# kv and M of a linear-attention block: from 6-head blocks on the whole array to 3-head blocks on 64-wide array tiles

## The chip, the cores and the metric

The kernel runs on one core of a Trainium2 chip. The metric is device time of one execution in microseconds (us); it is quoted as the median over runs. Engines in the profile: PE is TensorE's matmuls, PEld its weight loads, DVE VectorE, ACT ScalarE, POOL GpSimd, SP the engine that issues most DMAs (SPq is its queue). "Granted clock" is the share of TensorE's full clock in the records.

## The reference, cut to what matters

```python
def _A_ref(x, wqkv, wo):                     # B=1, S=2048, D=640, H=32 heads of 20
    q, k, v = ...                            # x @ wqkv, split into heads
    phi = lambda t: jnp.where(t > 0, t + 1, jnp.exp(t)) + 1e-6
    pq, pk = phi(q), phi(k)
    kv = jnp.einsum("bhsd,bhse->bhde", pk, v)      # 20 x 20 for each head
    z = jnp.einsum("bhsd->bhd", pk)
    o = jnp.einsum("bhqd,bhde->bhqe", pq, kv) / (den(pq, z) + 1e-6)
    return o @ wo
def _B_ref(x, w_gate, w_up, w_down):         # F = 1728
    return (gelu(x @ w_gate) * (x @ w_up)) @ w_down
g = sigmoid((x * gate_w).sum(-1, keepdims=True))
return g * _A_ref(...) + (1 - g) * _B_ref(...)
```

The kernel never forms `o`. It computes G = xᵀ·pk, then kv = wvᵀ·G for each head, then M = kv·wo (640 x 640), and puts (normalised pq)·M into the same accumulators as the FFN's last product. kv and M are the subject here. They are small: a head's kv is a 20 x 20 block on the diagonal of a 640 x 640 product.

## The kernel before: the parts that matter

Six heads (120 columns) are taken as one block. kv of a block is computed whole, 120 x 120, and everything off the 20 x 20 blocks is masked away. M of a block is one 120-row product in two halves of 320 columns. Its rows lie at multiples of 120, but the output stage wants them in tiles of 128 rows, so DMAs move them.

```python
    GH = 6; GW = GH * Dh; NG = 6             # 120 columns a block; the last block has 40
    def ps_tile(name):                       # one of the pool's 8 buffers (a "bank" below)
        return psum.tile([P, QW], FP32, name=name, tag="ps")
    ...
    def phase_KV(glo, ghi):
        kp = ps_tile("ps_kv")
        off = 0
        for g in range(glo, ghi):
            for ct in range(ND):             # ND = 5 tiles of 128 to contract over
                nc.tensor.matmul(
                    kp[0 : gw[g], off : off + gw[g]], lhsT=wv[:, ct, GW * g : GW * g + gw[g]],
                    rhs=g_sb[:, ct, GW * g : GW * g + gw[g]], start=(ct == 0), stop=(ct == ND - 1),
                )
            off += gw[g]
        ...                                  # kvt = kp * mask, on DVE
    def phase_M(g):
        ...
        for hh in range(2):
            cs = slice(hh * HALF, (hh + 1) * HALF)
            mp = ps_tile("ps_m")
            nc.tensor.matmul(mp[0 : gw[g], 0:HALF], lhsT=kvt[0 : gw[g], g, 0 : gw[g]],
                             rhs=wo_g[0 : gw[g], g, cs], start=True, stop=True)
            ...                              # cast to bf16: hh 0 on DVE, hh 1 on ACT
        ...                                  # 1 or 2 DMAs a block (10 in all) to rows of 128
    def phase_D(st):                         # normalise q, all on DVE, then a DMA transpose
        prod = work.tile([P, D], FP32, name="prod", bufs=2)
        nc.vector.tensor_tensor(out=prod[:], in0=pq[st][:], in1=zrep[:], op=ALU.mult)
        ...
    ...
    phase_Zrep()                             # the z product, "ps_z"
    phase_KV(0, 4)
    phase_E(1, 0)                            # FFN: 5 gate and 5 up matmuls, 128 x 512
    phase_KV(4, NG)
    ...
    phase_E(1, 1)
    phase_D(0)
    for ft in range(2, NF):
        phase_E(1, ft)
        if 0 <= ft - 3 < NG:
            phase_M(ft - 3)
        phase_D(ft - 1)
    for st in range(NF - 1, NT):
        phase_D(st)
    phase_FT(0)                              # first output stage: "ps_acc", then oT on DVE
```

## Time and profile before

| | before |
|---|---|
| time, median of the first 6 runs | 278.53 us (278.22 to 280.13) |
| PE busy, share of the span | 270.8 us, 98% |
| from the z product to the first output matmul (the "stretch" below) | 32.97 us |
| PE time of kv / of M in it | 1.69 us / 1.84 us |

The page's first and fourth parts say what bounds the kernel: busy us of each engine, and the shares of the chain of waits that ended last.

```profile
PE 270.8 (98%) x1462; PEld 136.5 (49%) x1487; DVE 146.9 (53%) x309; ACT 75.2 (27%) x155; POOL 3.7 (1%) x16
...
PE 96%; DMA 2%; issue 1%; SPq 0%; DVE 0%
```

PE is nearly always busy and is nearly the whole chain. What shortens PE's own work shortens the kernel, unless PE then has to wait.

The windows view of the stretch gives its length, then busy us (and instructions) of PE, PEld, DVE, ACT and POOL, then the granted clock, the DMA share and GB/s:

```profile
101.57:134.54 32.97, 32.76 (x178) 16.42 (x180) 31.81 (x63) 12.52 (x23) 0.00 (x0) 1.00 0.34 85
```

PE is busy 32.76 of 32.97 us, but DVE is too (31.81). DVE is the engine to watch for new waits.

The timeline of PE has one row per run of like instructions: start, us until the last one's modelled end, and what they are. To cost a stage, take starts alone, since the ends overlap with the next row. A 128x512 matmul starts 0.216 us after the one before it, so five take 1.08 us.

```profile
101.57 0.43 PE L262 MATMUL ps_z<-zsum,ones_bf 128*128 128x320 bf16 x2
101.84 1.26 PE L288 MATMUL ps_kv<-g_sb,wv 128*120 128x120 bf16 x20
102.94 1.24 PE L154 MATMUL ps_g<-xT_88,wg 128*128 128x512 bf16 x4
104.02 1.24 PE L154 MATMUL ps_u<-xT_88,wu 128*128 128x512 bf16 x5
105.10 0.66 PE L288 MATMUL ps_kv<-g_sb,wv 128*120 128x120 bf16 x10
105.69 0.60 PE L154 MATMUL ps_g<-xT_88,wg 128*128 128x512 bf16 x2
...
121.91 0.44 PE L316 MATMUL ps_m<-wo_g,kvt 120*120 120x320 bf16 x2
122.19 1.24 PE L154 MATMUL ps_g<-xT_88,wg 128*128 128x512 bf16 x4
123.27 1.24 PE L154 MATMUL ps_u<-xT_88,wu 128*128 128x512 bf16 x5
124.44 0.45 PE L316 MATMUL ps_m<-wo_g,kvt 40*40 40x320 bf16 x2
124.82 0.39 PE L154 MATMUL ps_g<-xT_88,wg 128*128 128x512 bf16 x1
```

kv: 101.84 to 102.94 and 105.10 to 105.69, together 1.69 us. M: a full block takes 0.27 to 0.28 us (121.91 to 122.19), five of them 1.37; the 40-row block takes from 123.27 + 1.08 = 124.35 to 124.82, 0.47 us, although its two matmuls need only 0.27. The other 0.2 us is lost where TensorE goes from 128*128 tiles to 40*40 ones and back: 0.09 us on each side (124.35 to 124.44 us, and 124.59 + 0.14 to 124.82). Sum: 3.53 us, 1.3% of the span. That is the ceiling of any change to kv and M.

### The profile page before, as it was taken

To read this page: it belongs to the slowest core of one execution; us is meant where nothing else is said; L and a number is where in the kernel's file an instruction comes from. 1 tells how busy PE (TensorE), PEld (TensorE's weight loads), DVE (VectorE), ACT (ScalarE), POOL (GpSimd) and SP (SyncE) were. 2 spreads that over 40 slices of the span, in tenths; PEclk is the share of its full clock that TensorE was granted. 3 is DMA by queue.
4 is the path that set the end of the run, shared out by engine and by line. 5 is a ranking of instruction groups with operands and counts; after the bars stand their busy time and mean duration, and the time that the engine had idled before them with its cause. 6 is when DMAs were issued, how large, how long until landed. Compare 5 with 4: busy or idle time off the path is not lost.

```text
span 277.1 us, 3820 instructions
## 1 busy us (share of the span) xinstructions
PE 270.8 (98%) x1462; PEld 136.5 (49%) x1487; DVE 146.9 (53%) x309; ACT 75.2 (27%) x155; POOL 3.7 (1%) x16
## 2 busy tenths in 40 slices
PE   7999999999999999999999999999999999999996
PEld 3554444555554494544444444444444444445675
DVE  0693323999998019999999863241122234111011
ACT  3572233644542252443100122220013222000100
POOL 4000000000000000000000000000000000000000
PEclk9999999999999999999999999999999999999999
DMA  6999999300000104343323352000132000011301
GB/s 199 357 357 202 241 350 279 128 0 2 0 0 4 1 2 137 68 105 77 61 47 45 74 99 95 2 0 19 38 40 95 0 0 2 19 38 34 125 24 47
DMA packets 43898, 23.64 MB, mean 85 GB/s; under 512 B 30825, under 2 KB 43753, under 8 KB 43881
## 3 DMA queue, kind: packets, MB, share of 16 engines
q1 hardware_dynamic: 43726, 23.25, 32.4%
q8 instruction: 11, 0.18, 0.3%
q10 hardware_dynamic: 154, 0.17, 0.2%
q14 instruction: 7, 0.05, 0.1%
HBM read 13.40 MB, written 2.63 MB: 58 GB/s over the span
## 4 chain that ended last, share of the span: by engine, by line
PE 96%; DMA 2%; issue 1%; SPq 0%; DVE 0%
PE ps_u L154 20%; PE ps_g L154 20%; PE ps_acc L363 15%; PE ps_kq L200 15%; PE ps_G L240 8%; PE ps_acc L360 6%; PE ps_acc L401 5%; PE ps_acc L398 2%; DMA wqk<-in_A_wqkv_dram 2%; PE ps_gu L154 2%; PE ps_k L200 1%; PE ps_acc L368 1%; PE ps_m L316 1%; PE ps_kv L288 1%; PE tp_x L145 0%
## 5 line engine op out<-in xcount | busy, mean ns | idle before, releaser
L159 ACT ACTIVATE gl<-ps_g 128x512 bf16<-128x512 f32 x52 | 31.1, 597 | 111.2 <-PE ps_g L154 111.2
L154 PEld LDWEIGHTS <-wu 128*128 128x128 bf16 x260 | 25.4, 98 | 30.7
L154 PEld LDWEIGHTS <-wg 128*128 128x128 bf16 x260 | 25.1, 98 | 29.1 <-issue 0.3
L160 DVE TENSOR_TENSOR hT_157<-ps_u,gl 128x512 bf16<-128x512 f32 x26 | 17.8, 689 | 29.5 <-PE ps_u L154 29.5
L363 PEld LDWEIGHTS <-wd 128*128 128x128 bf16 x195 | 19.1, 98 | 23.0
L363 PE MATMUL ps_acc<-hT_157,wd 128*128 128x512 bf16 x127 | 29.4, 379 | 0.2
L181 ACT ACTIVATE phi_e<-ps_kq 128x512 bf16<-128x512 f32 (+3 forms) x48 | 23.0, 505 | 21.2 <-PE ps_kq L200 19.1
L371 DVE TENSOR_TENSOR oT<-ps_acc,omg_rep 128x512 bf16<-128x512 f32 x15 | 10.4, 691 | 34.5 <-PE ps_acc L363 26.6
L160 DVE TENSOR_TENSOR hT_1249<-ps_u,gl 128x512 bf16<-128x512 f32 x26 | 17.8, 685 | 19.1 <-PE ps_u L154 19.1
L154 PE MATMUL ps_g<-xT_88,wg 128*128 128x512 bf16 x62 | 16.0, 379 | 0.2
L154 PE MATMUL ps_u<-xT_89,wu 128*128 128x512 bf16 x65 | 16.2, 379 | 0.0
L154 PE MATMUL ps_u<-xT_90,wu 128*128 128x512 bf16 x65 | 16.2, 379 | 0.0
L154 PE MATMUL ps_u<-xT_87,wu 128*128 128x512 bf16 x65 | 16.1, 379 | 0.0
L154 PE MATMUL ps_u<-xT_88,wu 128*128 128x512 bf16 x65 | 16.1, 379 | 0.0
L154 PE MATMUL ps_g<-xT_87,wg 128*128 128x512 bf16 x63 | 16.0, 379 | 0.1
L154 PE MATMUL ps_g<-xT_89,wg 128*128 128x512 bf16 x62 | 16.0, 379 | 0.2
L154 PE MATMUL ps_g<-xT_90,wg 128*128 128x512 bf16 x62 | 16.0, 379 | 0.2
L401 PE MATMUL ps_acc<-wd,hT_1249 128*128 128x320 bf16 (+2 forms) x120 | 15.9, 283 | 0.0
L240 PEld LDWEIGHTS <-x_all 128*128 128x128 bf16 x160 | 12.4, 98 | 7.1
L363 PE MATMUL ps_acc<-hT_1249,wd 128*128 128x512 bf16 x63 | 14.7, 379 | 0.1
L183 DVE TENSOR_SCALAR phi_m<-phi_e 128x512 bf16<-128x512 bf16 (+3 forms) x52 | 12.2, 258 | 2.1 <-ACT phi_e L181 1.9
L339 DVE TENSOR_REDUCE den<-prod 128x32 f32<-128x640 f32 x16 | 12.8, 801 | 0.0
(140 smaller groups left out, 290.8 us busy)
## 6 DMA issues: line engine op xcount, KB each, us to landing
wd<-in_B_w_down_dram SPq DMA_DIRECT2D x1, 2080.0 KB, 15.8
x_all<-in_A_x_dram SPq DMA_DIRECT2D x3, 640.0 KB, 5.9
out_dram<-o_q SPq DMA_DIRECT2D x3, 640.0 KB, 5.1
wg<-in_B_w_gate_dram SPq DMA_DIRECT2D x2, 640.0 KB
wu<-in_B_w_up_dram SPq DMA_DIRECT2D x2, 640.0 KB, 10.1
wqk<-in_A_wqkv_dram SPq DMA_DIRECT2D x1, 800.0 KB
wg<-in_B_w_gate_dram SPq DMA_DIRECT2D x1, 800.0 KB, 10.5
wu<-in_B_w_up_dram SPq DMA_DIRECT2D x1, 800.0 KB
```

What stands on the lines that cost most here:

```text
L154: nc.tensor.matmul(ps[:, t0 : t0 + tw], lhsT=w[:, dk, ft * P : (ft + 1) * P], rhs=xT[q][:, dk, t0 : t0 + tw], start=(dk == 0), stop=(dk == ...
L159: nc.scalar.activation(out=gl[:], in_=psg[:], func=ACT.Gelu_apprx_tanh)
L160: nc.vector.tensor_tensor(out=hT_cur[q][:, ft, :], in0=psu[:], in1=gl[:], op=ALU.mult)
L181: nc.scalar.activation(out=e[:, 0:w], in_=ps[:, 0:w], func=ACT.Exp)
L183: nc.vector.tensor_scalar(out=m[:, 0:w], in0=e[:, 0:w], scalar1=1.0, scalar2=EPS, op0=ALU.min, op1=ALU.add,)
L200: nc.tensor.matmul(ps[:, 0 : hi - lo], lhsT=xT[q][:, dk, sl * P : (sl + 1) * P], rhs=wqk[:, dk, lo:hi], start=(dk == 0), stop=(dk == ND - 1),)
L240: nc.tensor.matmul(gp[:, 0 : hi - lo], lhsT=x_all[:, st, ct * P : (ct + 1) * P], rhs=pk[st][:, lo:hi], start=(st == 0), stop=(st == NT - 1),)
L339: nc.vector.tensor_reduce(out=den[:], in_=prod[:].rearrange("p (h c) -> p h c", c=Dh), axis=AX.X, op=ALU.add)
L360: nc.tensor.matmul(acc[:], lhsT=M["all"][:, dk, ds], rhs=pqT[q][:, dk, :], start=(dt == 0 and dk == 0), stop=False)
L363: nc.tensor.matmul(acc[:], lhsT=wd[:, ft, ds], rhs=hT[:, ft, :], start=False, stop=(dt > 0 and ft == NF - 2))
L371: nc.vector.tensor_tensor(out=oT[:, 0:QW], in0=acc[:], in1=gsc["rep"][:, q * QW : (q + 1) * QW], op=ALU.mult)
L401: nc.tensor.matmul(acc[:, 0:w], lhsT=hT[:, ft, ts], rhs=wd[:, ft, lo:hi], start=False, stop=(ft == nf - 1 and (sl, h) != paired[0]))
```

## The change

Its intent: a 120-wide block wastes most of its kv (only 20 x 20 blocks are kept) and works the whole array (128*120 in the timeline). With 3-head blocks of 60, two kv matmuls are to run side by side in two column tiles of 64 (128*60), and four M matmuls (a quad) in four 64x64 tiles (60*64). The blocks of a pair of groups are laid out so that M's rows come out as whole blocks of 60. Fifteen DMAs instead of ten place them. kv is done in one piece, M in two lots, earlier than before. The core of the diff:

```diff
-    GH = 6
+    GH = 3
     GW = GH * Dh
     NG = 6
+    SUB = [(g, r, min(GW, D - GW * (2 * g + r))) for g in range(NG) for r in range(2) if GW * (2 * g + r) < D]
+    RP = P // 2
...
+    def phase_KV():
+        kps = [ps_tile("ps_kv") for _ in range(2)]
+        for g in range(NG):
             for ct in range(ND):
+                for gg, r, w in SUB:
+                    if gg == g:
+                        cs = slice(GW * (2 * g + r), GW * (2 * g + r) + w)
+                        nc.tensor.matmul(
+                            kps[r][RP * r : RP * r + w, GW * g : GW * g + w], lhsT=wv[:, ct, cs],
+                            rhs=g_sb[:, ct, cs], start=(ct == 0), stop=(ct == ND - 1),
+                        )
...
+    def phase_M(quads):
...
+        mps = {(q, r): ps_tile("ps_m") for q in quads for r in range(2)}
+        for pair, hh in quads:
+            for c in range(2):
+                for g, r, w in SUB:
+                    if g == 2 * pair + c:
+                        nc.tensor.matmul(
+                            mps[(pair, hh), r][RP * c : RP * c + RP, 0:HALF], lhsT=kvt[RP * r : RP * r + w, g, :],
+                            rhs=wo_g[RP * r : RP * r + w, g, hh * HALF : (hh + 1) * HALF], start=True, stop=True,
+                        )
...
-    phase_KV(0, 4)
     hT_cur[1] = ov.tile([P, NF, QW], BF16, name="hT1", tag="slab_b")
     phase_E(1, 0)
-    phase_KV(4, NG)
+    phase_KV()
...
-    phase_E(1, 1)
-    phase_D(0)
-    for ft in range(2, NF):
+    for ft in range(1, NF):
         phase_E(1, ft)
-        if 0 <= ft - 3 < NG:
-            phase_M(ft - 3)
-        phase_D(ft - 1)
-    for st in range(NF - 1, NT):
+        if ft == 1:
+            phase_M(((0, 0), (0, 1), (1, 0)))
+        elif ft == 2:
+            phase_M(((1, 1), (2, 0), (2, 1)))
+        else:
+            phase_D(ft - 3)
+    for st in range(NF - 3, NT):
         phase_D(st)
```

Cut: `wo_g` is loaded in two halves at partitions 0 and 64 (one DMA more), the mask and the zeroed `kvt` are made for 60-wide blocks, the casts of M go to ACT and DVE by `r`, and the placing DMAs.

More of the change, by code (lines that the diff above doesn't have):

```diff
@@ L42 @@
     HALF = D // 2
-    GH = 6
+    GH = 3
     GW = GH * Dh
     NG = 6
-    gw = [min(GW, D - GW * g) for g in range(NG)]
+    SUB = [(g, r, min(GW, D - GW * (2 * g + r))) for g in range(NG) for r in range(2) if GW * (2 * g + r) < D]
+    RP = P // 2
     NWARM = 6
@@ L78 @@
     wv = ov.tile([P, ND, D], BF16, name="wv", tag="slab_e")
-    wo_g = wpool.tile([GW, NG, D], BF16, name="wo_g")
+    wo_g = wpool.tile([P, NG, D], BF16, name="wo_g")
     wd = wpool.tile([P, NF, D], BF16, name="wd")
@@ L110 @@
     dma(out=wv[:], in_=wqkv_v[:, :, 2 * D : 3 * D])
-    dma(out=wo_g[:, 0 : NG - 1, :], in_=A_wo[0 : GW * (NG - 1), :].rearrange("(g p) n -> p g n", p=GW))
-    dma(out=wo_g[0 : gw[-1], NG - 1, :], in_=A_wo[GW * (NG - 1) : D, :])
+    wo_v = A_wo[0 : 2 * GW * (NG - 1), :].rearrange("(g r p) n -> r p g n", r=2, p=GW)
+    for r in range(2):
+        dma(out=wo_g[RP * r : RP * r + GW, 0 : NG - 1, :], in_=wo_v[r])
+    dma(out=wo_g[0 : SUB[-1][2], NG - 1, :], in_=A_wo[2 * GW * (NG - 1) : D, :])
     dma(out=wd[:, 0 : NF - 1, :], in_=B_w_down[0:FM, :].rearrange("(k p) n -> p k n", p=P))
@@ L120 @@
                          rhs=nc.const_aps.tensor(1.0, [P, QW], BF16), start=(r == 0), stop=(r == NWARM - 1))
-    NGB = 4
-    mask = consts.tile([GW, NGB * GW], BF16, name="mask")
+    mask = consts.tile([P, NG * GW], BF16, name="mask")
     nc.gpsimd.memset(mask[:], 1.0)
-    mv = mask[:].rearrange("p (g h c) -> p g h c", g=NGB, h=GH)
-    nc.gpsimd.affine_select(
-        out=mv, in_=mv, pattern=[[0, NGB], [-Dh, GH], [0, Dh]],
-        compare_op=ALU.is_ge, fill=0.0, base=0, channel_multiplier=1,
-    )
-    nc.gpsimd.affine_select(
-        out=mv, in_=mv, pattern=[[0, NGB], [Dh, GH], [0, Dh]],
-        compare_op=ALU.is_ge, fill=0.0, base=Dh - 1, channel_multiplier=-1,
-    )
+    for r in range(2):
+        mv = mask[RP * r : RP * r + RP, :].rearrange("p (g h c) -> p g h c", g=NG, h=GH)
+        nc.gpsimd.affine_select(
+            out=mv, in_=mv, pattern=[[0, NG], [-Dh, GH], [0, Dh]],
+            compare_op=ALU.is_ge, fill=0.0, base=0, channel_multiplier=1,
+        )
+        nc.gpsimd.affine_select(
+            out=mv, in_=mv, pattern=[[0, NG], [Dh, GH], [0, Dh]],
+            compare_op=ALU.is_ge, fill=0.0, base=Dh - 1, channel_multiplier=-1,
+        )
     eneg = consts.tile([P, NT], FP32, name="eneg")
@@ L279, in phase_gate @@
         gsc["omg"] = omg_all
-    kvt = consts.tile([GW, NG, GW], BF16, name="kvt")
-    def phase_KV(glo, ghi):
-        kp = ps_tile("ps_kv")
-        off = 0
-        for g in range(glo, ghi):
-            for ct in range(ND):
-                nc.tensor.matmul(
-                    kp[0 : gw[g], off : off + gw[g]], lhsT=wv[:, ct, GW * g : GW * g + gw[g]],
-                    rhs=g_sb[:, ct, GW * g : GW * g + gw[g]], start=(ct == 0), stop=(ct == ND - 1),
-                )
-            off += gw[g]
-        off = 0
-        full = [g for g in range(glo, ghi) if gw[g] == GW]
-        n = len(full)
+    kvt = consts.tile([P, NG, RP], BF16, name="kvt")
@@ new lines @@
+    nc.gpsimd.memset(kvt[:], 0.0)
+    def phase_KV():
+        kps = [ps_tile("ps_kv") for _ in range(2)]
+        for g in range(NG):
+            for ct in range(ND):
+                for gg, r, w in SUB:
[4 more added lines that the diff above has]
+                            rhs=g_sb[:, ct, cs], start=(ct == 0), stop=(ct == ND - 1),
+                        )
+        for r in range(2):
+            rs = slice(RP * r, RP * r + GW)
+            n = NG - 1
+            nc.vector.tensor_tensor(
+                out=kvt[rs, 0:n, 0:GW], in0=kps[r][rs, 0 : n * GW].rearrange("p (g c) -> p g c", g=n),
+                in1=mask[rs, 0 : n * GW].rearrange("p (g c) -> p g c", g=n), op=ALU.mult,
+            )
+        w = SUB[-1][2]
@@ L296, in phase_KV @@
         nc.vector.tensor_tensor(
-            out=kvt[:, glo : glo + n, :], in0=kp[0:GW, 0 : n * GW].rearrange("p (g c) -> p g c", g=n),
-            in1=mask[:, 0 : n * GW].rearrange("p (g c) -> p g c", g=n), op=ALU.mult,
-        )
-        if n < ghi - glo:
-            w = gw[-1]
-            nc.vector.tensor_tensor(
-                out=kvt[0:w, NG - 1, 0:w], in0=kp[0:w, n * GW : n * GW + w], in1=mask[0:w, 0:w], op=ALU.mult,
-            )
-    M = {}
-    def phase_M(g):
-        if g == 0:
-            M["all"] = ov.tile([P, ND + NG, D], BF16, name="m_all", tag="slab_c")
-        m_sb = M["all"][:, 0:ND, :]
-        m_st = M["all"][:, ND : ND + NG, :]
-        for hh in range(2):
-            cs = slice(hh * HALF, (hh + 1) * HALF)
-            mp = ps_tile("ps_m")
-            nc.tensor.matmul(mp[0 : gw[g], 0:HALF], lhsT=kvt[0 : gw[g], g, 0 : gw[g]],
-                             rhs=wo_g[0 : gw[g], g, cs], start=True, stop=True)
-            if hh == 0:
-                nc.vector.tensor_copy(out=m_st[0 : gw[g], g, cs], in_=mp[0 : gw[g], 0:HALF])
-            else:
-                nc.scalar.copy(out=m_st[0 : gw[g], g, cs], in_=mp[0 : gw[g], 0:HALF])
-        lo = GW * g
-        hi = lo + gw[g]
-        while lo < hi:
-            k = lo // P
-            e = min(hi, (k + 1) * P)
-            dma(out=m_sb[lo - k * P : e - k * P, k, :], in_=m_st[lo - GW * g : e - GW * g, g, :])
-            lo = e
@@ new lines, in phase_KV @@
+            out=kvt[0:w, NG - 1, 0:w], in0=kps[0][0:w, (NG - 1) * GW : (NG - 1) * GW + w],
+            in1=mask[0:w, 0:w], op=ALU.mult,
+        )
+    M = {}
+    def phase_M(quads):
+        if not M:
+            m_all = ov.tile([P, ND * D + NG * D], BF16, name="m_all", tag="slab_c")
+            M["sb"] = m_all[:, 0 : ND * D].rearrange("p (k n) -> p k n", k=ND)
+            M["st"] = m_all[:, ND * D :].rearrange("p (s n) -> p s n", s=NG)
+        mps = {(q, r): ps_tile("ps_m") for q in quads for r in range(2)}
[6 more added lines that the diff above has]
+                            rhs=wo_g[RP * r : RP * r + w, g, hh * HALF : (hh + 1) * HALF], start=True, stop=True,
+                        )
+        for pair, hh in quads:
+            for r in range(2):
+                h = RP if 2 * (2 * pair + 1) + r >= len(SUB) else P
+                (nc.vector.tensor_copy if r else nc.scalar.copy)(
+                    out=M["st"][0:h, 2 * pair + r, hh * HALF : (hh + 1) * HALF], in_=mps[(pair, hh), r][0:h, 0:HALF])
+            if hh == 0:
+                continue
+            for g, r, w in SUB:
+                if g // 2 != pair:
+                    continue
+                lo = base = GW * (2 * g + r)
+                while lo < base + w:
+                    k = lo // P
+                    e = min(base + w, (k + 1) * P)
+                    o = RP * (g % 2) - base
+                    dma(out=M["sb"][lo - k * P : e - k * P, k, :], in_=M["st"][o + lo : o + e, 2 * pair + r, :])
+                    lo = e
@@ L359, in phase_FT @@
             for dk in range(ND):
-                nc.tensor.matmul(acc[:], lhsT=M["all"][:, dk, ds], rhs=pqT[q][:, dk, :],
+                nc.tensor.matmul(acc[:], lhsT=M["sb"][:, dk, ds], rhs=pqT[q][:, dk, :],
                                  start=(dt == 0 and dk == 0), stop=False)
@@ L397, in phase_F3 @@
                     for dk in range(ND):
-                        nc.tensor.matmul(acc[:, 0:w], lhsT=pqT[q][:, dk, ts], rhs=M["all"][:, dk, lo:hi],
+                        nc.tensor.matmul(acc[:, 0:w], lhsT=pqT[q][:, dk, ts], rhs=M["sb"][:, dk, lo:hi],
                                          start=(head and dk == 0), stop=False)
```

## The prediction

278.53 us less 1.2 us of PE time, plus most of the allowance of 0.3 + 0.2 us, gives 277.7. The 64-row matmuls are the case of row tiles: in the trace of before two start at 138.521 and 138.524 us, the next two at 138.747 and 138.751.

> **What bounds the kernel.** TensorE. The page gives PE busy 270.8 of 277.1 us (98%), and the chain that ended last is 96% PE. By the windows view DVE is busy 36.0 of 36.0 us between 104 and 140 us, where kv, M and the normalisation of q (phase_D) run, but PE does not wait for it.
>
> **What the changed parts cost now, on PE** (timeline, start to start).
> - kv: 20 matmuls of 128x120 at 55 ns, later 5 more, then five with 40 columns at 25 ns, with about 0.1 us lost going into the narrow array tile and 0.1 us coming out: 1.10 + 0.59 = 1.69 us.
> - M: five groups of two 120x320 matmuls, 0.27 us each; the 40-row group 0.47 us, again with 0.1 us lost on each side: 1.83 us.
> Sum 3.5 us, 1.3% of the span, all on the chain: no version of this change reaches 2% by itself.
>
> **What the change does to that.**
> - kv becomes 55 matmuls of at most 60 columns, alternating between two column tiles. [...] pairs of 64-row matmuls in the output stage start 3 to 4 ns apart and share one 0.21 us slot. If column tiles do the same: 30 slots of 28 ns + 0.2 us for the switches = 1.05 us (-0.65). If one after another: 55 x 27 ns + 0.2 = 1.7 us, nothing gained.
> - M becomes 22 matmuls on 64x64 tiles in six quads. If four overlap, a quad is 0.14 us: 0.85 us, plus two stays in the tiled mode at 0.2 us (now one): 1.25 us (-0.6). [...]
> Expected PE saving 1.2 us; 0.5 to 0.6 if column tiles don't overlap.
>
> **Off PE.** Twelve casts of M (ACT 0.43, DVE 0.48 us) and three mask products (about 1.1 us) stay. 15 DMAs instead of 10 place M, 0.75 us of the queue each; M is ready by about 125 us, its first reader starts at 134 us: hidden. POOL has more mask work, but idles 4.6 us before the piece that matters (8.18 us).
>
> **New waits.** M now follows the second FFN pair instead of the fourth, and takes six of eight PSUM banks twice. The masks must be done 2.1 us after kv, and six casts in 2.2 us; both just fit (slack about 1 and 0.4 us) unless 0.8 us pieces of phase_D get in between on DVE. I allow 0.3 us for that, and 0.2 us for column tiles that do not overlap. DVE's backlog ends as before at about 157 us; oT frees banks 1.7 us before PE needs them, so a PE 1.2 us earlier still fits, barely.
>
> **Prediction.** 277.7 us, range 276.8 to 278.9. Faster by over 2%: 0.01; within 2%: 0.98; slower by over 2%: 0.01.
>
> **What would show it.** Right: kv pairs 3 to 4 ns apart in the timeline, 28 ns per pair; quads of M starting within 12 ns; kv + M near 2.3 us; no idle of PE above 0.2 us between 101 and 115 us. Wrong: 25 to 30 ns per single kv matmul; PE waiting for kvt, for casts of M or, near 155 us, for oT.
>
> **What would make it wrong.** DVE order: if phase_D no longer starts at 102.7 us, DVE idles, its backlog ends up to 5 us later, and PE waits for banks around 157 us.

## The result, and the profile after

The changed kernel took 277.65 us, the median of 10 runs (277.17 to 279.39), against 278.38 us for before, the median of 20 (278.09 to 280.13). The ratio is 0.9981, 95% interval 0.9958 to 1.0004: the same within 2%. Ratios here are the mean time of one kernel's fast runs over that of the other's of the same rounds, so not quite the ratio of the quoted medians.

Both kernels' times fall into two groups, 1.7 to 1.8 us apart, all called fast, since they are within 1.5%. Over all runs, 42 of 51 runs of before lie below 279 us (median 278.37) and 9 between 279.9 and 281.1. Of the changed kernel's 16, 11 lie below 277.8 (median 277.31) and 5 between 278.9 and 279.4. Group for group it is 1.06 us faster. Nine of 51 against five of 16 is too few to say that the change makes the upper group more frequent. Taken over all kernels there is no sign of it: 13 of 63 runs of the three kernels that work on the whole array, 10 of 61 of those with tiled kv (the slow run of kv_serial left out). What the upper group is comes below.

The same lines of the profile after: the page's busy times (its chain is 96% PE again), and in the second fence the windows view of the stretch, now 101.02 to 132.83 us.

```profile
PE 268.7 (98%) x1496; PEld 134.1 (49%) x1522; DVE 146.9 (53%) x309; ACT 74.8 (27%) x155; POOL 4.8 (2%) x19
```

```profile
101.02:132.83 31.81, 31.49 (x213) 14.65 (x215) 30.59 (x60) 12.14 (x23) 0.00 (x0) 1.00 0.39 87
```

The stretch is 1.16 us shorter, 31.81 against 32.97 us. DVE has as much to do as before in the whole span (146.9 us).

The timeline of PE from the z product on:

```profile
101.02 0.43 PE L265 MATMUL ps_z<-zsum,ones_bf 128*128 128x320 bf16 x2
101.30 1.24 PE L157 MATMUL ps_g<-xT_88,wg 128*128 128x512 bf16 x4
102.38 1.24 PE L157 MATMUL ps_u<-xT_88,wu 128*128 128x512 bf16 x5
103.55 1.05 PE L294 MATMUL ps_kv<-g_sb,wv 128*60 128x60 bf16 x55
104.76 1.03 PE L157 MATMUL ps_g<-xT_88,wg 128*128 128x512 bf16 x4 [0.16 <-issue]
105.62 1.24 PE L157 MATMUL ps_u<-xT_88,wu 128*128 128x512 bf16 x5
106.80 0.60 PE L323 MATMUL ps_m<-wo_g,kvt 60*64 60x320 bf16 x12
107.33 1.25 PE L157 MATMUL ps_g<-xT_88,wg 128*128 128x512 bf16 x5
108.42 1.24 PE L157 MATMUL ps_u<-xT_88,wu 128*128 128x512 bf16 x5
109.59 0.60 PE L323 MATMUL ps_m<-wo_g,kvt 60*64 60x320 bf16 x10
110.17 0.38 PE L157 MATMUL ps_g<-xT_88,wg 128*128 128x512 bf16 x1
```

kv runs from 102.38 + 1.08 = 103.46 to 104.54 us (the row of gate matmuls after it has four of five records; its first start is 104.76 - 0.22). That is 1.09 us for 55 matmuls. M takes 106.70 to 107.33 and 109.50 to 110.17, 1.30 us for 22. Sum 2.39 in place of 3.53 us. So kv gave 0.60 and M 0.54 us, nearly all of the 1.16. PE does not wait for the masks or the casts: each stay (one uninterrupted piece of work on a part of the array) begins 0.09 us after the FFN's last slot, as the 40-row block's did in before.

Single starts show the overlap. These are read from the trace record by record, in us, for kv from the second pair on (not a view of the profile):

```
kv, changed kernel:  103.599 103.602 | 103.629 103.632 | 103.659 103.662 | 103.689 103.692 ...
M, first lot:        106.795 106.799 106.802 106.805 | 106.955 106.959 106.962 106.965 | 107.091 107.094 107.098 107.101
```

kv's matmuls go in pairs, 3 ns apart and 30 ns from pair to pair. M's go in fours, 3 to 4 ns apart; the second four starts 160 ns after the first, the third 136 ns after the second.

Two things outside the stretch also differ between the two traces: the changed kernel's started 0.55 us earlier, and its end took 0.13 us longer. 1.16 + 0.55 - 0.13 = 1.58 us is what the spans differ by (277.07 and 275.50). The experiments deal with both.

### The profile page after: what moved, and what is told of

It reads as the page before. It is cut to its first block, busy times and chain, and to the rows that moved or that the text cites. A ratio compares the mean times of both kernels' runs of the same rounds, so it can differ in the third digit from the quotient of the medians.

```text
span 275.5 us, 3900 instructions
## 1 busy us (share of the span) xinstructions
PE 268.7 (98%) x1496; PEld 134.1 (49%) x1522; DVE 146.9 (53%) x309; ACT 74.8 (27%) x155; POOL 4.8 (2%) x19
## 4 chain that ended last, share of the span: by engine, by line
PE 96%; DMA 2%; issue 1%; SPq 0%; DVE 0%
PE ps_g L157 20%; PE ps_u L157 20%; PE ps_acc L378 15%; PE ps_kq L203 15%; PE ps_G L243 8%; PE ps_acc L375 6%; PE ps_acc L416 5%; PE ps_acc L413 2%; DMA wqk<-in_A_wqkv_dram 2%; PE ps_gu L157 2%; PE ps_k L203 1%; PE ps_acc L383 1%; PE ps_m L323 0%; PE ps_kv L294 0%; PE tp_x L148 0%
## 5 line engine op out<-in xcount | busy, mean ns | idle before, releaser
L416 PEld LDWEIGHTS <-hT_1231 128*128 128x128 bf16 x120 | 11.0, 98 | 3.5
```

The costliest lines, as they stand in the source:

```text
L416: nc.tensor.matmul(acc[:, 0:w], lhsT=hT[:, ft, ts], rhs=wd[:, ft, lo:hi], start=False, stop=(ft == nf - 1 and (sl, h) != paired[0]))
```

## The experiments

The theory: the gain is array tiles working at once. Rivals: the new order interrupts the FFN less often; smaller blocks are cheaper by themselves; or the difference lies in the start and not in the change. The table gives, for each trace, the start of the first q/k product of the main loop (first start of "ps_kq"), the stretch, the time from the first matmul of the third FFN quarter (the FFN takes the 2048 rows in four quarters of 512) to the last matmul's modelled end, and the tail from there to the end of the span. Times are of all timed runs; "before" in the same batches was 278.45 to 278.52 us.

| kernel | time, median us (runs) | q/k start | stretch | third FFN quarter on | tail |
|---|---|---|---|---|---|
| before | 278.38 (20) | 9.89 | 32.97 | 119.50 | 2.75 |
| changed | 277.65 (10) | 9.31 | 31.81 | 119.50 | 2.88 |
| before_again | 278.50 (6) | 9.60 | 32.97 | 119.50 | 2.75 |
| after_again | 277.33 (6) | 9.32 | 31.81 | 119.50 | 2.89 |
| order_only | 278.53 (6) | 9.84 | 32.96 | 119.50 | 2.76 |
| kv_serial_again | 278.23 (4) | 9.85 | 32.46 | 119.50 | 2.89 |
| kv_run5 | 277.54 (6) | 9.57 | 31.80 | 119.50 | 2.89 |
| m_serial | 277.69 (6) | 9.39 | 32.06 | 119.50 | 2.89 |
| m_six | 278.51 (6) | 9.22 | 32.69 | 119.50 | 2.88 |
| m_whole | 277.35 (6) | 9.08 | 32.20 | 119.50 | 2.69 |
| after_dve4 | 279.00 (6) | 9.77 | 31.80 | 121.04 | 2.89 |
| before_dve4 | 279.43 (6) | 11.08 | 32.97 | 119.63 | 2.76 |
| after_tail | 277.21 (6) | 9.69 | 31.80 | 119.50 | 2.69 |

The stretch, the later part and the tail come back within 0.01 us in both programs that were traced twice. The start does not. So a change of a tenth of a microsecond is read here from a stage of the trace, and not from run times. The medians also mix the two groups of run times: m_six, m_whole, after_dve4 and after_tail have no run in the upper one, kv_run5 and m_serial have two of six. Lower group against the changed kernel's lower group (277.31), kv_run5 is 0.22 us slower, m_serial 0.28, kv_serial_again 0.92 and m_six 1.20: the order of the stretches, but up to 0.3 us off.

### before_again and after_again: how much of the difference is chance

No edit; both kernels once more.

> The kernel before, unchanged, for a second trace of it. The first pair of traces differs by 1.6 us, of which only 1.15 us lies in kv and M; 0.55 us lies before 10 us from the start (first weights land at 6.8 us in the one and 6.2 us in the other). If that start is chance, the start of the first q/k product moves by some 0.5 us between traces of the same kernel. If the change caused it, this trace starts as the first trace of before did (9.9 us). The stretch from the z product to the first output matmul should be 32.97 us again, within 0.05 us. Some runs will be about 1.8 us slower than the rest (3 of 20 so far).

> The changed kernel, unchanged. If the start is chance: its q/k products may start anywhere between 9.3 and 9.9 us. If the change caused it: at 9.3 us again. The stretch from the z product to the first output matmul should be 31.81 us again, within 0.05 us. Runs 1.8 us slower than the rest were 4 of 10; if the change makes them more frequent they stay near 4 of 10, if not they fall towards the share of before.

Measured: 278.50 us and 277.33 us (ratio of the changed kernel to before in this batch 0.996, interval 0.9929 to 0.9991). The stretches repeat within 0.01 us. The start moves, 9.60 us against 9.89 for before, and over all traces between 9.1 and 9.9 us (and once 11.08) whatever the kernel: the changed kernel's family has 9.31, 9.32, 9.85, 9.57, 9.39, 9.22, 9.77 and 9.69. The early start of the first trace of the changed kernel lies within this spread. Its second trace started as early (9.32), so two traces alone would not show chance; but the run times of the lower groups differ by 1.06 us, and the stretch and the tail already give 1.16 - 0.13 = 1.03, which leaves the start next to nothing.

### order_only: the new order without the new tiles

```diff
-    phase_KV(0, 4)
     hT_cur[1] = ...
     phase_E(1, 0)
+    phase_KV(0, 4)
     phase_KV(4, NG)
...
+    for ft in range(1, NF):
+        phase_E(1, ft)
+        if ft <= 2:
+            for g in range(3 * (ft - 1), 3 * ft):
+                phase_M(g)
+        else:
+            phase_D(ft - 3)
```

> 6-head blocks on the whole array as before, but in the order of the changed kernel: all of kv after the first FFN pair, M in two lots of three groups after the second and third. Theory (the gain is the overlap of array tiles): kv 1.7 and M 1.8 us of PE as before, the stretch from the z product to the first output matmul stays 32.9 to 33.0 us, time as before within 0.2 us. Rival (the gain comes from the new order, fewer interruptions of the FFN): the stretch falls to about 31.8 us and the time by 1.1 us.

Measured: 278.53 us, ratio to before 1.0002 (0.9964 to 1.0040), stretch 32.96 us. Its timeline row for kv, and the one after:

```profile
103.96 1.76 PE L288 MATMUL ps_kv<-g_sb,wv 128*120 128x120 bf16 x30
105.65 1.25 PE L154 MATMUL ps_g<-xT,wg 128*128 128x512 bf16 x5
```

From 103.96 to 105.65, kv takes 1.69 us in one piece as it did in two, and the stretch as a whole is unchanged. The order is worth nothing; that rival is out.

### kv_serial: the same kv matmuls, one column tile after the other

```diff
-        for g in range(NG):
-            for ct in range(ND):
+        for rr in range(2):
+            for g, ct in [(g, ct) for g in range(NG) for ct in range(ND)]:
                 for gg, r, w in SUB:
-                    if gg == g:
+                    if gg == g and r == rr:
```

> The changed kernel with the same 55 kv matmuls, but all 30 of column tile 0 first, then all 25 of column tile 1, so that neighbours never lie on different tiles. Theory: they run one after another at 27 to 30 ns each: kv takes 55 x 28 ns + 0.2 us = 1.75 us in place of 1.09, the stretch and the time grow by 0.6 to 0.7 us against the changed kernel, and the whole gain from kv is gone. Rival (the gain is from the smaller blocks themselves, not from neighbours on different tiles): kv stays near 1.1 us, no change of time.

The first time its profiled run took 359.13 us: of the 128x512 matmuls two in three started 266 ns after the last and one in three 318 ns, instead of 216, while the durations on DVE were the usual ones. What slowed it was not found. It says nothing of the change and is left out; the other five runs took 277.86 to 279.73 us. So it was run again.

> The same kernel as kv_serial, for a trace at the full clock (that trace fell in a run in which a 128x512 matmul took 266 ns instead of 216). Theory: 55 kv matmuls at 27 to 30 ns each and 0.2 us for the switches, 1.75 us in place of 1.09; the stretch from the z product to the first output matmul 31.81 + 0.66 = 32.5 us. Rival (block size alone matters): kv stays near 1.1 us and the stretch at 31.8 us, and the 0.75 us by which its timed runs were slower come from elsewhere.

Measured: 278.23 us, stretch 32.46 us, 0.65 us longer than the changed kernel's. Its timeline row:

```profile
104.05 1.74 PE L294 MATMUL ps_kv<-g_sb,wv 128*60 128x60 bf16 x55
105.72 0.60 PE L157 MATMUL ps_g<-xT,wg 128*128 128x512 bf16 x2
```

The same 55 matmuls take 1.74 us instead of 1.05, one every 30 ns. That is as long as kv took in one piece on the whole array (1.76 us in order_only). Smaller blocks bring nothing alone; the whole gain of kv is the overlap of the two column tiles.

### m_serial: M's matmuls, one tile after the other

```diff
-        for pair, hh in quads:
-            for c in range(2):
+        for c, rr in ((0, 0), (0, 1), (1, 0), (1, 1)):
+            for pair, hh in quads:
                 for g, r, w in SUB:
-                    if g == 2 * pair + c:
+                    if g == 2 * pair + c and r == rr:
```

> The changed kernel with the same 22 M matmuls, ordered so that matmuls on one 64x64 tile follow each other (three of them, then the next tile). Theory: of 12 and 10 matmuls only the ones at the change of tile overlap, which leaves 9 and 7 slots of 0.136 us where there were 3 and 3: 10 x 0.136 = 1.36 us more PE time, stretch from the z product to the first output matmul 33.2 us, time 1.3 us above the changed kernel. Rival (the hardware finds the free tile by itself, or the order does not matter): no change.

This expectation failed. Measured: 277.69 us, stretch 32.06 us: 0.25 us longer and not 1.36.

```profile
106.85 0.75 PE L323 MATMUL ps_m<-wo_g,kvt 60*64 60x320 bf16 x12
107.53 1.25 PE L157 MATMUL ps_g<-xT,wg 128*128 128x512 bf16 x5
108.62 1.24 PE L157 MATMUL ps_u<-xT,wu 128*128 128x512 bf16 x5
109.80 0.63 PE L323 MATMUL ps_m<-wo_g,kvt 60*64 60x320 bf16 x10
```

The built program does have the matmuls in the order of the edit: three on one tile, three on the next, and so on. They still overlap: the row of twelve lasts 0.75 us, against 0.60 in the changed kernel. Twelve matmuls fit into four slots, where one after another with overlap only at a change of tile would need nine. In the second lot the program ends with two 40-row matmuls on one tile and, as the tenth, a 60-row one on the last tile. In the record the last to start is a 40-row one, at 110.134 us, and four of the ten start in the first slot (109.797, 109.807, 109.834 and 109.844). The marks of semaphores that the records carry say which is which: the third and the fourth to start are the seventh and the tenth of the program. So in this run a matmul on another tile started ahead of earlier ones. Of the 0.25 us, 0.15 is the fourth slot of the first lot; the other 0.10 is no matter of tiles but a wait of PE behind the second lot, where the next up matmul (111.56 us) waits for the product hT on DVE (done at 111.51 us).

### kv_run5: kv in rows of five on one column tile

In kv_serial_again the first matmul of column tile 1 already started (104.856 us) while three of tile 0 were still to come (104.875, 104.900, 104.926), and its second (104.908) came before the last of these. So starts out of order occur on column tiles too, but with thirty matmuls in a row only a few overlap (1.74 us for the 55, against 1.05). This run has rows of five.

```diff
         for g in range(NG):
-            for ct in range(ND):
-                for gg, r, w in SUB:
+            for gg, r, w in SUB:
+                for ct in range(ND):
                     if gg == g:
```

> The changed kernel with kv's matmuls in runs of five on one column tile, then five on the other. m_serial showed that TensorE starts matmuls on a free tile ahead of earlier ones that wait for a busy tile, and kv_serial that it does so for only some three or four matmuls. Theory (it looks a few matmuls ahead): overlap is partial, kv takes 1.1 to 1.35 us, the stretch 31.8 to 32.1 us. Rival (column tiles overlap only when neighbours alternate, and M overlapped in m_serial because its tiles lie on different rows): kv takes 1.65 us or more, stretch 32.4 us.

Measured: 277.54 us, stretch 31.80 us, the same as with strict alternation.

```profile
103.80 1.05 PE L294 MATMUL ps_kv<-g_sb,wv 128*60 128x60 bf16 x55
104.78 1.04 PE L157 MATMUL ps_g<-xT,wg 128*128 128x512 bf16 x4
```

The overlap is full, not partial as expected. Runs of five on one tile cost nothing, runs of 25 and 30 cost nearly all of it; where in between the limit lies was not measured.

### m_six: M in six stays instead of two

```diff
-        if ft == 1:
-            phase_M(((0, 0), (0, 1), (1, 0)))
-        elif ft == 2:
-            phase_M(((1, 1), (2, 0), (2, 1)))
-        else:
+        if ft <= 6:
+            phase_M((divmod(ft - 1, 2),))
+        if ft >= 3:
             phase_D(ft - 3)
```

> The changed kernel with M in six lots of one quad, after each of six FFN pairs, in place of two lots of three. Theory: the same six slots of 0.136 us but six stays in the tiled mode instead of two, at 0.2 us each: 0.8 us more, stretch 32.6 us, time 0.8 us above the changed kernel; about 0.07 us of M's gain is left. Rival (switches cost nothing when the FFN is around them): no change.

Measured: 278.51 us, stretch 32.69 us, 0.88 us longer than the changed kernel's.

```profile
108.05 1.24 PE L157 MATMUL ps_u<-xT,wu 128*128 128x512 bf16 x5
109.22 0.33 PE L323 MATMUL ps_m<-wo_g,kvt 60*64 60x320 bf16 x4
109.48 0.82 PE L157 MATMUL ps_g<-xT,wg 128*128 128x512 bf16 x3
```

From the end of the FFN's slot, 108.05 + 1.08 = 109.13, to its next start at 109.48 is 0.35 us for a quad that needs 0.136. Each stay on the small tiles costs 0.2 us here, and four stays more cost the 0.88. In the changed kernel about 0.1 us lies going in (103.46 to 103.55 us, kv) and 0.1 us coming out (107.09 + 0.14 to 107.33 us, M). With one quad per stay M takes 1.30 + 0.88 = 2.18 us, more than the 1.84 of before: the two lots of three, which take six PSUM banks each, are what makes tiling pay for M.

### m_whole: kv tiled, M on the whole array

```diff
-    kvt = consts.tile([P, NG, RP], BF16, name="kvt")
+    kvt = consts.tile([P, NG, 2 * GW], BF16, name="kvt")          # zero outside the two 60 x 60 blocks
+    nc.vector.memset(wo_g[:], 0.0)                                # rows that no block uses
...
+        for g in quads:
+            for hh in range(2):
+                mp = ps_tile("ps_m")
+                nc.tensor.matmul(mp[0 : 2 * GW, 0:HALF], lhsT=kvt[:, g, :], rhs=wo_g[:, g, cs], start=True, stop=True)
```

Cut: the masks write the two blocks of 60 into one of 120, the casts and the placing DMAs are those of 6-head blocks again, and three small tiles of phase_D (den, dtmp, rg) have two buffers in place of three.

> The changed kernel with kv as changed (3-head blocks on two column tiles) but M as before: two 3-head blocks side by side, padded with zeros, as one 6-head block on the whole array, twelve matmuls of 128x120 by 320 columns, in the changed order, placed by 10 DMAs. It isolates M's part of the gain and needs no mode switch for M. Theory: 12 x 0.136 = 1.63 us for M in place of 1.27, so the stretch from the z product to the first output matmul is 31.81 + 0.36 = 32.17 us and the time 0.35 us above the changed kernel, still 0.75 us below before. Together with kv_serial (0.65 us) and the last group's switch (0.2 us) that would account for the gain of 1.16 us. Rival (M has the larger part of the gain): stretch 32.4 us or more.

Measured: 277.35 us, stretch 32.20 us, 0.39 us longer than the changed kernel's.

```profile
106.48 1.03 PE L324 MATMUL ps_m<-wo_g,kvt 128*120 128x320 bf16 x6
107.34 1.24 PE L158 MATMUL ps_g<-xT,wg 128*128 128x512 bf16 x5
...
109.50 0.98 PE L324 MATMUL ps_m<-wo_g,kvt 128*120 128x320 bf16 x6
110.31 1.03 PE L158 MATMUL ps_g<-xT,wg 128*128 128x512 bf16 x4
```

M takes 0.88 + 0.81 = 1.69 us here, 1.30 in the changed kernel and 1.84 in before. Of M's gain of 0.54 us, 0.15 comes from not having a narrow last block with its own switch, and 0.39 from the four tiles, net of two stays. Its time is no worse than that of the changed kernel's lower group (277.35 and 277.31), although the stretch is longer: 0.19 us of the 0.39 come back in its shorter tail (2.69 us), and the rest is within the spread of the start.

### after_dve4 and before_dve4: how much slack VectorE has

Four of the sixteen normalisation steps of q do their first product twice.

```diff
-        nc.vector.tensor_tensor(out=prod[:], in0=pq[st][:], in1=zrep[:], op=ALU.mult)
+        for _ in range(2 if 8 <= st < 12 else 1):
+            nc.vector.tensor_tensor(out=prod[:], in0=pq[st][:], in1=zrep[:], op=ALU.mult)
```

> The changed kernel with four useless VectorE products of 128x640 (0.73 us of pitch each, 2.9 us in all) put into the normalisation of q, tiles 8 to 11, where VectorE is full. It is to tell how much slack is left before TensorE waits for the banks that oT frees: the trace of the changed kernel has the first oT done at 155.98 us, and TensorE needs a fourth bank at 156.35 us. Theory (0.3 us of slack left): VectorE ends 2.9 us later, TensorE waits about 2.5 us early in the third FFN quarter, time 2.5 us above the changed kernel. Rival (VectorE is off the path with room to spare, or the schedule finds other banks): no change.

Measured: 279.00 us. From the third FFN quarter on it takes 121.04 us instead of 119.50: 1.54 us more, not 2.5. The timeline of after_dve4:

```profile
158.67 0.69 DVE L387 TENSOR_TENSOR oT<-ps_acc,omg_rep 128x512 bf16<-128x512 f32 x1
159.28 0.81 DVE L365 TENSOR_TENSOR pq<-pq,rg 128x640 bf16<-128x640 bf16 x1
159.41 1.24 PE L157 MATMUL ps_g<-xT,wg 128*128 128x512 bf16 x5 [1.38 <-DVE oT L387]
```

PE sits idle for 1.38 us until the first oT is done, which frees a PSUM bank. The wait is the one that was foreseen, but the slack is larger: the row that waits is the fifth tile of that quarter, since the third quarter began at 153.56 us and 153.56 + 4 x 1.08 = 157.88. Added work 4 x 0.73 = 2.92 us, wait 1.54: the changed kernel has 1.4 us of slack.

> The kernel before with the same four useless VectorE products as in after_dve4. There TensorE waited 1.54 us for the bank of the first oT: 2.9 us of added work less 1.4 us of slack, since the fifth tile of the third FFN quarter needs that bank and not, as I had taken it, the fourth. In before, the fifth tile starts at 154.82 + 4 x 1.08 = 159.14 us and the first oT is done at 156.28 us: 2.86 us of slack. Theory: the added 2.9 us just use it up, TensorE waits 0.1 us, time within 0.3 us of before. Rival (the wait in after_dve4 is of another kind, not spent slack): the same 1.5 us here.

Measured: from the third quarter on 119.63 us, 0.13 us more than 119.50, as expected. Before has 2.8 us of slack, the changed kernel 1.4. Counted from the z product, PE comes 1.16 us earlier to that point, and the first oT starts 0.25 us later (155.29 - 101.02 = 54.27 against 155.59 - 101.57 = 54.02). The change spent half of the slack and did not reach the wall. By these numbers a further 1.4 us off PE before this point would run into it (an estimate).

The time of before_dve4, 279.43 us, is that high because three of its six runs are in the upper group (280.16 to 280.26), the profiled one among them. That trace shows what sets it apart. Its first k products on PE:

```profile
4.85 1.06 PE L200 MATMUL ps_k<-wqk,xT 128*128 128x512 bf16 x2
6.25 1.86 PE L200 MATMUL ps_k<-wqk,xT 128*128 128x512 bf16 x4 [0.35 <-DMA wqk<-in_A_wqkv_dram]
...
8.17 2.23 PE L200 MATMUL ps_k<-wqk,xT 128*128 128x512 bf16 x9
```

The same rows of the changed kernel's trace, which is in the lower group:

```profile
4.52 0.67 PE L203 MATMUL ps_k<-wqk,xT_87 128*128 128x512 bf16 x2
6.21 1.02 PE L203 MATMUL ps_k<-wqk,xT_87 128*128 128x512 bf16 x4 [1.03 <-DMA wqk<-in_A_wqkv_dram]
...
7.28 1.35 PE L203 MATMUL ps_k<-wqk,xT_87 128*128 128x512 bf16 x9
```

The weights come at the same time (6.25 and 6.21 us), but the matmuls after it start every 427 ns and not every 216. That lasts until about 10 us: the last matmul with a pitch (start to start) of 427 ns begins at 9.42 us, and the trace's own record of the clock has the full clock from 10.06 us on. In the ten traces of the lower group that hold such a record it begins between 3.6 and 5.9 us (5.62 in before, 3.73 in the changed kernel). The q/k products start 1.8 us later than in the changed kernel's trace (11.08 and 9.31 us), 1.2 to 1.5 later than in the other traces of before (9.60 and 9.89). Why some runs start so was not tried. One trace of the upper group is all there is, so that every run of the group is of this kind is not shown; and its page still gives the granted clock as 1.0.

### after_tail: the end of the program

After the last matmul SP waits for the completion of its last DMAs, one wait after another. Starts of these waits after the start of the last matmul, in us, read from the records:

| kernel | DMAs against before | waits of SP | behind the last landing |
|---|---|---|---|
| before | 0 | 1.02, 1.08, 1.46, 2.09, 2.15 | 1 |
| m_whole | +1 | 1.02, 1.08, 1.14, 1.45, 2.09 | 0 |
| changed | +6 | 1.48, 2.10, 2.16, 2.22, 2.28 | 3 |

The wait that the last landing ends is at 2.09 or 2.10 us in each. What follows in line costs 0.06 us each. The records of before (79 DMAs) and of the changed kernel (85) name eight semaphores for their landings, one after another in a fixed turn. The last output has the semaphore of the fourth of the five waits in before, and of the second in the changed kernel.

```diff
-    dma(out=wd[:, 0 : NF - 1, :], in_=...)
+    for lo, hi in ((0, 4), (4, 7), (7, 10), (10, NF - 1)):
+        dma(out=wd[:, lo:hi, :], in_=wd_v[:, lo:hi, :])
```

> The changed kernel with the load of w_down cut into four DMAs in place of one, three DMAs more and nothing else. At the end SP goes through the completion waits of its last DMAs in a fixed order, 0.06 us each; in before one wait stands behind that for the last output DMA to land, in the changed kernel (six DMAs more) three, in m_whole (one more) none. Theory (each DMA takes the next of the completion semaphores in turn, eight of them, so the number of DMAs decides where the last one stands): three more DMAs leave none behind it, the tail after the last matmul falls from 2.88 to 2.69 us, the stretch from the z product stays 31.81 us, and the time is 0.2 us below the changed kernel, about 277.1 us in its faster runs. Rival (the longer tail has to do with the memory or the DMA traffic of the changed kernel): tail stays at 2.88 us.

Measured: 277.21 us (277.11 to 277.45), tail 2.69 us, waits at 1.02, 1.08, 1.14, 1.45 and 2.09. The number of DMAs sets the tail in these kernels: with 0, 1, 6 and 9 more than before, 1, 0, 3 and 0 waits stand behind the last landing, which fits the turn of eight in the records. This version has the changed kernel's stretch and the shortest tail, 0.2 us less by the trace. It is the fastest median, ratio to before 0.9945 (0.9919 to 0.9972). None of its six runs fell into the upper group, which flatters that ratio; against the lower group of the changed kernel it is 0.1 us faster (277.21 and 277.31), half of the 0.2 expected; the run times do not resolve that, since that lower group spreads from 277.12 to 277.79.

## Why the prediction was right

277.7 us was predicted and 277.65 measured, within the range and in the class foreseen. The mechanism held. The agreement to 0.05 us is luck, and two terms were wrong.

- **What bounds it: right.** PE's time in kv and M fell by 1.14 us and the stretch by 1.16.
- **kv: right.** 1.05 us foreseen with overlap, 1.09 measured; 0.65 us of gain foreseen, 0.60 measured, and kv_serial_again gives 0.65 back. Pairs 3 ns apart as foreseen, 30 ns for a pair instead of 28.
- **M: right.** 1.25 us foreseen, 1.30 measured, quads within 10 ns. m_six confirms 0.2 us for each stay.
- **"I allow 0.3 us for that, and 0.2 us for column tiles that do not overlap": neither happened.** PE waited for no mask and no cast, and the column tiles overlap fully. Without this allowance the sum was 278.53 - 1.2 = 277.3 us, which is what the lower group does (median 277.31); that this fits so well is luck too, since 278.53 lies 0.16 above the lower group of before (278.37) and so makes up for the tail below, which was not foreseen. With the whole allowance the sum would have been 277.8. The median of the first ten runs came out at 277.65 because four of them were in the upper group.
- **Not foreseen: the tail.** Six more DMAs moved two waits behind the last landing, +0.13 us. 1.16 - 0.13 = 1.03 us is the net gain by the traces, and the lower groups differ by 1.06.
- **"oT frees banks 1.7 us before PE needs them, so a PE 1.2 us earlier still fits, barely": mis-sized.** I took the fourth tile of the next FFN quarter for the one that needs the bank. It is the fifth, as the wait in after_dve4 shows (I take it that a gelu has given a bank back by then). The slack was 2.8 us in before and is 1.4 us now.
- **"If phase_D no longer starts at 102.7 us": it still does** (102.18 us in the changed kernel), so the case foreseen for a wrong prediction did not arise.

## What to carry to other kernels

Count first what share of the bounding engine's time the changed part has: 3.5 of 277 us could never be more than 1.3%, however well the tiles overlap. Array tiles paid here when several small matmuls shared one stay: two of kv ran in 30 ns, four of M in 0.14 to 0.16 us, and a stay cost 0.2 us. The order within a stay hardly mattered with rows of three matmuls (M, 0.15 us) or five (kv, nothing) on one tile; rows of 25 and 30 cost 0.65 us. When differences are of 0.1 to 1 us, compare single stages of the traces, which repeat to 0.01 us, and look for two groups in the run times before trusting a median.
